# An adaLN block kernel: own PSUM banks in the last product, a one-column 1+ca, a mean shared with ScalarE, and a new order

## Chip, cores and metric

The kernel runs on one core of a Trainium2 chip. The metric is the device time of one launch in microseconds, the median of several runs; lower is better. A core has TensorE (matrix products, PE in the profile), VectorE (DVE), ScalarE (ACT), GpSimd (POOL) and SyncE (SP), which here issues all DMAs from one queue. Each engine works through its own instructions in order and waits at an instruction until what it needs is there. Matrix products write into PSUM, which has eight banks of 512 fp32 columns in each of its 128 partitions.

## What is computed

One transformer block with sequence 2048 and width 512, modulated by a conditioning vector c:

```python
mod = silu(c) @ w_mod                       # six rows: sa, ca, ga, sb, cb, gb
h = layernorm(x) * (1 + ca) + sa
q, k, v = split(h @ wqkv)                   # 32 heads of 16
pq, pk = phi(q), phi(k)                     # phi(t) = where(t > 0, t + 1, exp(t)) + 1e-6
kv, z = einsum(pk, v), sum(pk)              # linear attention: 16 x 16 per head
x = x + ga * ((pq @ kv / (pq @ z)) @ wo)
h = layernorm(x) * (1 + cb) + sb
u = gelu(h @ w_in)                          # 1376 columns: z1 and z2, 688 each
g = w_sp @ layernorm(z2) + b_sp             # mixing along the sequence, 2048 x 2048
x = x + gb * ((z1 * g) @ w_out)
```

## The kernel before

Rows are handled in 16 tiles of 128. Nearly every large operand is split into two halves, a high part rounded to the fast matrix format (fp32r) and a low part, the rest; a product a·b is then three products, high·high, high·low and low·high (mm3, lines 117 to 119). The high part is written by ScalarE, the low part by VectorE or GpSimd. A few small products run in plain fp32, as two instructions each.

The program is a list of short tokens. Two strings, ORDER (first part) and ORDER3 (second part), name some 1,800 steps by two letters and indices; run_all walks through them and emits each step's instructions, DMAs among them, in that order to the engines' queues. Tiles live in numbered slots of pools; the strings in SLOTS say which slot a tile takes at each turn. A step that writes into a slot or a PSUM tile waits until the readers of what was there before are done. A reader and a writer of one PSUM tile wait for each other even where they touch different columns of it.

The steps that matter below, by stage:

- **Start.** load_m (lm), load_wk/load_w (lw), load_xt (ly) and load_x (lx) load the parts of w_mod for sa and ca, the weights, the turned and the plain rows. dummy (du) runs products of ones into a scratch bank. col_mm (cm, line 201) makes 1+ca as a column: 16 fp32 products of 128 x 128 blocks of w_mod with the activated c, spread over 128 columns; col_end (ce) and mean_col (mc, line 333) read it. mean_mm (mr, line 339) makes the mean rows of w_k and w_q over their inputs, four products of 512 columns each, which w_mid (wf, line 343) subtracts from (1+ca)·w. w_hi and w_lo (qh, qd, qg) split the result. k_part (ki, kj, line 424) and k_mm, q_mm (km, qm) are the first products with the split weights; turn_hi and turn_lo (th, tl) split the turned rows. mod_prod and mod_add (yp, ya), then col_part (cr, line 208), make the column of sa, with one-column products.
- **Attention.** gm sums h·pk over all tiles into G. kv_mm and kv_mask (kv, kx) make the masked 16 x 16 blocks. m2_mm (mm0 to mm3, tile pm) multiplies them by wo; two of the four share a PSUM tile, m2_evac (me) takes each out as two halves. a_t and a_te (at, ae) turn and split pq for tiles 0 to 3, wo_mm (wo) is the product po, x1_out (x1) adds it to x.
- **Gated MLP, first product.** h2, then turning by TensorE (ht) or by DMA (hp, hm), splitting (hh, hl), and z_mm (z0, z1, line 661). Tiles 12 to 15 of z1 come late: z_late and z1_late (zw, zg, lines 858 and 864). mod_bcast (mB) makes the last modulation row; mB5 is the last use of the first part's PSUM pools.
- **Mixing along the sequence.** A seven-product scheme over pairs of row blocks: t_diff, t_hi, t_lo and s_sum, s_hi, s_lo (td, th, tl; ss, fh, fl, fg) prepare the operands, prod (pr p,h,k, line 942, tile P) multiplies, c_sum and c_end (cs, cd) combine. u_mul, u_planes, u_x, u_merge, u_sum, u_park (um, up, ux, ug, ua, uq) turn the gated rows and park them in DRAM; u_back, u_hi, u_lo (ur, uh, ul) bring them back and split them.
- **Last product.** Also by seven products for each pair of row blocks p: o_prod (op p,k) and o_rest (or p,n) write four outputs of 256 columns, numbered b,c, by o_mm (line 1127, tile pout); o_add (oa p,n, line 1150) adds them to the rows on VectorE, some of them in the middle of an accumulation (oa p,0 after op p,1; oa p,1 after op p,6; oa p,3 after op p,7; oa p,2 after op p,5), and stores finished rows. The two outputs of one b share a bank; p takes banks 2p+7 and 2p+8, modulo 8. wout_hi and wout_lo (oh, os) split the weights of this product.

The late part's eight banks are given out by bank(k); before, bank k lies at the address of the k-th bank *first used*, zw13's banks 2 and 3 at the first two, where the first part's pool of one-bank tiles "t" lies.

Of the kernel before, what the change touches and what calls it, by code (L numbers as in the profile page):

```python
# [28 lines left out]
def block_kernel(ctx: ExitStack, tc: tile.TileContext, x, x_t, w_qkv, w_o, w_in, w_sp, b_sp, w_out,  # L29
# [166 lines left out]
    def col_mm(m, kc):  # L196
        if m not in CP:
            CP[m] = ps("t", [P, KC, P], f"pcol{m}")
        for i in range(KC):
# [1 line left out]
            mm(CP[m][:, i], RAW["mod", m, kc // 2][:, kc % 2, i * P:(i + 1) * P],
               sil[:, kc:kc + 1].to_broadcast([P, P]), start=n == 1, stop=n == KC * KC, skip_group_check=True)
# [128 lines left out]
    def mean_col():  # L331
        WC["c"] = sb("tb", [P, KC, P], F32, "cbr")
        nc.scalar.activation(WC["c"], CP[1], AF.Copy, scale=1.0 / D, bias=1.0 / D)

    def mean_mm(j, kc):
        if j not in WC:
            WC[j] = ps("t", [P, D], f"wm{j}")
# [1 line left out]
        mm(WC[j], WC["c"][:, kc], w_raw(j, kc), start=n == 1, stop=n == KC)

# [429 lines left out]
    def hx_lo(t):  # L770
# [21 lines left out]
        cr0 qg0,2 ly4 qg0,0 s10 ce0 ly11 kr2 by0 km5 th3 kj1,3 lw2,1 bh0 lx6 s11 bp1 kj0,2 bp3 by1 by2 bp0 qm0
        by3 bp2 ba1 kj0,0 s15 ly6 bx1 lx4 qr0 kr1 tl3 ki0,2 bb1 be1 ka2 ly7 bh1 k15 ba2 kr0 bh2 qm1 ba3 km3
        bx0 lx7 qr1 qm3 ka0 bl0 s13 lw2,0 ka1 lx8 k20 k40 k22 ly8 kr3 kh0 mV2,0 k42 th4 kh2 lx10 bb0 k25 bl2
        lo0 bh3 bh5 ly10 kl0 be0 mV2,1 qm2 ks0 bl1 ly12 tl4 k45 k21 th9 th6 kl2 lx9 ly13 ly14 k41 kh1 ks1 gm0
        bl5 q13 q12 kl1 mS2 bl3 ka3 gm2 th11 tl6 qm4 tl11 kh5 ks2 gm1 lx11 q22 s16 q23 mB2 kl5 tl9 q42 bh6 s14
# [15 lines left out]
        g20 wo5 ht1 hl2 d16 q415 d110 z12 d27 x14 he1 g22 d112 ap7 hm3 z01 lX5 d26 d210 hh3 zl2 g11 am8 ap6
        z02 hl3 h24 d19 g12 z13 ah8 am7 z11 hp4 lX10 am6 ah6 lX8 d212 ah7 g23 g21 al7 x15 zl3 h25 wo7 zl0 z03
        d113 hm4 zn3 lX6 al6 d29 wo6 al8 hh4 ap10 hl4 hp5 d115 zn0 z14 wo8 x17 d213 zh3 x16 ap9 z04 h27 d111
        hm5 zn2 am10 g13 d215 ah10 hh5 ap12 hl5 al10 d211 wo10 hp7 x18 g24 am9 g14 d114 h28 hm7 zl1 z15 x110
# [447 lines left out]
```

## Time and profile before

| | |
|---|---|
| median of 3 runs | 626.55 us (625.43 to 627.54) |
| profiled execution, its own time | 624.86 us |
| its span, first to last instruction | 623.1 us |
| TensorE, busy | 606.1 us (97%) |
| TensorE weight loads, busy | 561.9 us (90%) |
| VectorE / ScalarE / GpSimd, busy | 497.7 / 370.7 / 236.8 us |
| DMA | 109.99 MB, mean 177 GB/s |
| mean granted TensorE clock | 0.993 |

A profile row "PE pm L117 <- DVE m L135: 4.0, 2, 2.5" in the view of waits reads: TensorE's instructions of line 117 that write pm waited for VectorE's instructions of line 135 that write m, 4.0 us in all, 2 times, 2.5 us the longest. In a timeline a row has the start and the duration in us, the engine, line, operation, output and inputs, the shape and the number of instructions; in brackets the idle time before it and what ended it. In the view by groups a row has busy time and mean duration in ns, then the idle time before. In the view by stretches a row has the stretch, its length, then busy time and number of instructions of TensorE, its weight loads, VectorE, ScalarE and GpSimd, and the granted clock, the busy share of the DMA engines and their rate. The chain is what ended last, followed back step by step.

### The profile page before, as it was taken

The numbers are of one execution on the slowest core, as the hardware profiler recorded it, in microseconds if no ns is written. First come the engines' busy times: TensorE is split into PE (matmuls) and PEld (weight loads), VectorE is DVE, ScalarE is ACT, GpSimd is POOL, SyncE is SP. The second block draws the span as 40 slices with busy tenths as digits, with TensorE's granted clock in tenths as the row PEclk, the third lists the DMA queues.
The fourth block names the chain that finished last, engine by engine and source line by source line (L and its number), as shares of the span: only waits on it lengthen the run. The fifth ranks groups of instructions, "written<-read, shape, count | busy, mean of one in ns | idle before, by whom it ended". The sixth has DMA issues, their size and how long they took to land.

```text
span 623.1 us, 9978 instructions
## 1 busy us (share of the span) xinstructions
PE 606.1 (97%) x3542; PEld 561.9 (90%) x3542; DVE 497.7 (80%) x933; ACT 370.7 (59%) x629; POOL 236.8 (38%) x208
## 2 busy tenths in 40 slices
PE   9999999999799999999999999999999999999997
PEld 7688888888589999899999999999999999989997
DVE  2998988896678878898969896866768687998765
ACT  2796594656446564757738455546565667776421
POOL 0842542737865575456422012303121312232320
PEclk9999999999899999999999999999999999999999
DMA  8242520523225546777566926365756848899973
GB/s 324 98 153 85 186 84 23 192 78 125 80 62 147 163 124 193 181 218 240 159 243 234 310 76 188 77 193 143 200 156 174 273 139 231 264 303 259 342 220 120
DMA packets 91027, 109.99 MB, mean 177 GB/s; under 512 B 57088, under 2 KB 57600, under 8 KB 90976
## 3 DMA queue, kind: packets, MB, share of 16 engines
q1 hardware_dynamic: 90976, 109.35, 57.9%
q8 instruction: 28, 0.46, 0.3%
q14 instruction: 23, 0.19, 0.1%
HBM read 68.17 MB, written 28.05 MB: 154 GB/s over the span
## 4 chain that ended last, share of the span: by engine, by line
PE 84%; DMA 5%; DVE 5%; ACT 2%; POOL 2%; issue 1%; SPq 1%; ACTq 0%; POOLq 0%; DVEq 0%
PE P L942 30%; PE z L661 14%; PE pout L1127 9%; PE z L858 2%; PE qp L117 2%; PE qp L118 2%; PE g L119 2%; PE qp L119 2%; PE g L118 2%; PE g L117 2%; PE kp L119 2%; PE kp L117 2%; PE kp L118 2%; PE po L117 2%; PE po L119 2%; PE po L118 2%
## 5 line engine op out<-in xcount | busy, mean ns | idle before, releaser
L942 PE MATMUL P<-z,f 128*128 128x344 f32 x768 | 125.8, 320 | 0.9 <-ACT z L864 0.9
L942 PEld LDWEIGHTS P<-z,f 128*128 128x128 f32 x768 | 121.8, 188 | 1.2 <-ACT z L864 1.1
L929 POOL TENSOR_TENSOR f<-raw_wsp,f 128x512 fp32r<-128x512 f32 x32 | 46.8, 1468 | 170.3 <-ACT f L926 114.6
L661 PE MATMUL z<-win,ht 128*128 128x344 f32 x672 | 107.8, 320 | 0.6 <-DVE ht L305 0.6
L661 PEld LDWEIGHTS z<-win,ht 128*128 128x128 f32 x672 | 106.3, 188 | 1.7 <-DVE ht L305 0.9
L1127 PE MATMUL pout<-wout,ut 128*128 128x256 f32 (+1 forms) x448 | 56.9, 284 | 4.1 <-DVE x L1150 4.0
L1127 PEld LDWEIGHTS pout<-wout,ut 128*128 128x128 f32 (+1 forms) x448 | 54.6, 189 | 5.6 <-DVE x L1150 2.9
L926 ACT ACTIVATE f<-raw_wsp 128x512 fp32r<-128x512 f32 x64 | 39.2, 626 | 29.4 <-PE P L942 20.3
L261 POOL TENSOR_TENSOR mv<-ve,mhalf 128x1 f32<-128x1 f32 x48 | 35.5, 746 | 37.7 <-DVE ve L260 22.0
L926 ACT ACTIVATE f<-sa 128x512 fp32r<-128x512 f32 x48 | 29.8, 628 | 31.1 <-PE P L942 20.5
L929 DVE TENSOR_TENSOR f<-sa,f 128x512 fp32r<-128x512 f32 x48 | 34.2, 719 | 15.2 <-ACT f L926 15.0
L285 ACT COPY uca<-ucb 128x768 uint16<-128x768 uint16 x32 | 32.0, 1069 | 6.6 <-DMA ucb<-uca 6.6
L483 POOL TENSOR_TENSOR pksum<-pksum,tk 128x512 f32<-128x512 f32 x15 | 22.6, 1506 | 34.2 <-DVE tk L455 34.0
L1150 DVE TENSOR_TENSOR x<-x,pout 128x256 f32<-128x256 f32 (+1 forms) x49 | 23.3, 498 | 15.3 <-PE pout L1127 15.1
L1030 ACT ACTIVATE ut<-ur 128x512 fp32r<-128x512 f32 x32 | 18.9, 625 | 22.9 <-DMA ur<-ud 14.9
L590 POOL TENSOR_TENSOR prod<-pq,zrep 128x512 f32<-128x512 f32 x16 | 20.7, 1304 | 22.6 <-DVE den L598 12.0
L929 DVE TENSOR_TENSOR f<-raw_wsp,f 128x512 fp32r<-128x512 f32 x32 | 22.7, 712 | 8.2 <-ACT f L926 8.1
L1039 POOL TENSOR_TENSOR ut<-ur,ut 48x128 fp32r<-48x128 f32 x16 | 11.4, 714 | 43.7 <-ACT ut L1030 43.7
L275 ACT COPY uca<-us 128x768 uint16<-128x768 uint16 x32 | 25.0, 827 | 4.7 <-PE P L942 2.8
L117 PE MATMUL po<-m,pt 128*128 128x512 f32 x64 | 26.1, 408 | 0.0
L119 PE MATMUL po<-m,pt 128*128 128x512 f32 x64 | 25.8, 402 | 0.0
L118 PE MATMUL po<-m,pt 128*128 128x512 f32 x64 | 25.7, 402 | 0.0
(254 smaller groups left out, 1513.6 us busy)
## 6 DMA issues: line engine op xcount, KB each, us to landing
raw_wsp<-in_w_sp SPq DMA_DIRECT2D x32, 512.0 KB, 4.3
ud<-uca SPq DMA_DIRECT2D x16, 512.0 KB, 4.7
ur<-ud SPq DMA_DIRECT2D x16, 512.0 KB, 5.3
z1d<-z SPq DMA_DIRECT2D x16, 344.0 KB, 2.6
zd<-zz SPq DMA_DIRECT2D x16, 344.0 KB, 2.7
z1r<-z1d SPq DMA_DIRECT2D x16, 344.0 KB, 4.1
xt<-in_x_t SPq DMA_DIRECT2D x16, 256.0 KB, 3.8
x<-in_x SPq DMA_DIRECT2D x16, 256.0 KB, 3.3
```

What stands on the lines that cost most here:

```text
L117: mm(o, a_hi, b_hi, start=first, stop=False, **kw)
L118: mm(o, a_hi, b_lo, start=False, stop=False, **kw)
L119: mm(o, a_lo, b_hi, start=False, stop=last, **kw)
L261: nc.gpsimd.tensor_tensor(mv[:, 1:2], ve, mhalf, op=OP.pow)
L275: nc.scalar.copy(pl[:, h], v[:, :, h])
L285: copy(o[:, :, h], plt[:, h * n:(h + 1) * n].rearrange("p a b -> p (a b)"))
L661: mm(p[:, b, :HB], a[:, i, kc], win[h][:, j, kc, b * HB:(b + 1) * HB], start=kc == 0 and k == 0, stop=kc == KC - 1 and k == 2)
L926: nc.scalar.activation(SF[p, h, k][:, 0], s_src(p, h, k), AF.Copy)
L929: eng.tensor_sub(SF[p, h, k][:, 1], s_src(p, h, k), f(SF[p, h, k][:, 0]))
L942: mm(B[p, k][:, :HB], a[:, x_], t[:, y_], start=n == 1, stop=n == 24)
L1127: mm(o_bank(p, b, c), a, w, start=NPO[k] == 1, stop=last, skip_group_check=True)
L1150: nc.vector.tensor_add(o, o, PO[p, b][:, k:k + c1 - c0])
```

## The change

1. 1+ca is made with one column per product instead of 128; mean_col spreads it while reading.
2. The mean row of w_q takes only inputs 0 and 1 (of four blocks) by mean_mm. Blocks 2 and 3 are scaled on ScalarE (ms, mp), added on GpSimd (ma), split (mx) and summed over partitions by two fast products with ones into the same bank (mb).
3. The late part's banks lie in sequence: bank k at address k.
4. Each 256-column output of the last product has a bank of its own: p takes four banks from 4p+7 on, modulo 8. An add of 512 columns becomes two of 256.
5. SLOTS, ORDER and ORDER3 are new. The new steps ms, mp2, mp3, ma2,3, mx2 and mb come in, mr0,2 and mr0,3 go; all other steps are the same, in another order.

```diff
     def col_mm(m, kc):
         if m not in CP:
-            CP[m] = ps("t", [P, KC, P], f"pcol{m}")
+            CP[m] = ps("t", [P, KC], f"pcol{m}")
...
-            mm(CP[m][:, i], RAW["mod", m, kc // 2][:, kc % 2, i * P:(i + 1) * P],
-               sil[:, kc:kc + 1].to_broadcast([P, P]), start=n == 1, stop=n == KC * KC, skip_group_check=True)
+            mm(CP[m][:, i:i + 1], RAW["mod", m, kc // 2][:, kc % 2, i * P:(i + 1) * P],
+               sil[:, kc:kc + 1], start=n == 1, stop=n == KC * KC, skip_group_check=True)
...
-        nc.scalar.activation(WC["c"], CP[1], AF.Copy, scale=1.0 / D, bias=1.0 / D)
+        nc.scalar.activation(WC["c"], CP[1][:, :, None].to_broadcast([P, KC, P]), AF.Copy, scale=1.0 / D, bias=1.0 / D)
...
+    def mean_scale():
+        WC["s"] = const.tile([P, KC], F32, name="cas")
+        nc.scalar.activation(WC["s"], CP[1], AF.Copy, scale=1.0 / D, bias=1.0 / D)
+
+    def mean_prod(kc):
+        WC["p", kc] = sb("tb", [P, D], F32, f"wp{kc}")
+        nc.scalar.activation(WC["p", kc], w_raw(0, kc), AF.Copy, scale=WC["s"][:, kc:kc + 1])
+
+    def mean_add(a, b):
+        nc.gpsimd.tensor_add(WC["p", a], WC["p", a], WC["p", b])
+
+    def mean_split(a):
+        WC["h"] = sb("s4", [P, 2, D], F32R, "wph")
+        hi_lo(WC["h"][:, 0], WC["h"][:, 1], WC["p", a])
+
+    def mean_row():
+        for h in range(2):
+            n = WC["n", 0] = WC["n", 0] + 1
+            mm(WC[0], ones, WC["h"][:, h], start=False, stop=n == KC)
...
     psp = late.enter_context(tc.tile_pool(name="psp", bufs=1, space=PSUM, reuse_waits="tile"))
+    for k in range(8):
+        psp.tile([P, 512], F32, tag=f"bank{k}", name=f"bank_{k}")
...
     def o_bank(p, b, c):
-        if (p, b) not in PO:
-            PO[p, b] = bank((2 * p + 7 + b) % 8, f"pout{p}_{b}")
-        return PO[p, b][:, 256 * c:256 * c + 256]
+        if (p, b, c) not in PO:
+            PO[p, b, c] = bank((4 * p + 7 + 2 * b + c) % 8, f"pout{p}_{b}{c}", (P, 256))
+        return PO[p, b, c]
...
-        nc.vector.tensor_add(o, o, PO[p, b][:, k:k + c1 - c0])
+        for c in range(c0, c1, 256):
+            v = X3[2 * p + t][:, c:c + 256]
+            nc.vector.tensor_add(v, v, PO[p, b, (k + c - c0) // 256])
```

Of the two order strings, the places that the prediction speaks of (old, then new):

```diff
-        lm1,0 lm1,2 lm1,3 du1 du4 si du2 lm1,1 du3 cm1,0 ly1 cm1,2 lw1,0 lw1,1 cm1,3 cm1,1 ce1 ly0 lw0,1 lw0,0
-        du5 lm0,1 mc mr1,1 th1 mr1,0 lm0,0 th0 mr1,3 ly5 ly2 mr1,2 mr0,2 lm0,2 tl1 tl0 mr0,3 wf1,3 wf1,1 wf1,0
-        lm0,3 qh1,3 qh1,1 wf1,2 mr0,0 qg1,3 mr0,1 qh1,0 qd1,0 ki0,1 wf0,1 qg1,1 kj0,3 yp0,1 lx0 ki0,3 wf0,3
+        ly1 lm1,0 lm1,1 du1 du2 du3 si lm1,2 cm1,0 lm1,3 du4 lw1,0 ly5 cm1,1 cm1,2 cm1,3 lw1,1 th1 tl1 du5 ms
+        lw0,1 mc ce1 th5 mp2 lw0,0 mr1,1 ly0 lx0 tl5 mp3 mr1,3 th0 mr1,0 ma2,3 ly2 mr1,2 wf1,3 mr0,0 wf1,2
+        wf1,1 wf1,0 mr0,1 qh1,3 lm0,2 mx2 th2 lx2 tl0 qg1,3 qh1,2 qh1,1 lm0,1 mb qh1,0 qg1,1 lm0,0 s10 yp0,2
...
-        d13 gh0 wh0,3 d22 gh1 d11 gh3 kv0 gh2 d20 d21 kv1 d18 kv3 vb kv2 d23 lX2 at2 wl0,3 wh1,1 kx d28 qm15
-        lX4 q115 d15 at0 qm14 ae0 q114 ae2 mm0 mm2 me0 lW1,2 wh1,0 wl1,0 d14 mm1 at1 me1 me2 mm3 wl1,1 at3 me3
-        wo0 ae3 ae1 d17 d24 wl0,2 ap4 wo3 x10 wh1,2 x13 wo1 wh1,3 w02 wl1,3 h20 ht0 w12 d25 he0 ap5 q215 lX7
+        wh0,2 gh1 gh0 d12 lW1,0 d10 d13 gh3 d22 kv0 gh2 mB4 d20 vb d11 kv3 d23 kv1 lX0 kv2 wh0,3 at2 wh1,1 d18
+        lW1,3 kx qm15 mm2 wl0,3 wl1,1 mm0 at0 ae2 q115 wh1,2 d21 ae0 d14 qm14 d15 wl0,2 me2 me0 at3 mm1 d28
+        q114 mm3 at1 me1 ae1 me3 ae3 wh1,0 wo0 wo3 d24 wh1,3 ap4 wl1,0 x10 x13 wo1 wl1,3 q214 h20 w02 d25 q414
...
-        zp15 tl1,5 zh15 zw12 zp13 tl2,5 ss0,0,4 zt12 zg12 zh12 fh0,1,2 zh13 td0 tl2,6 fh0,0,7 zt14 zg13 zo15
-        th1,6 zh14 fh0,0,3 ss0,1,1 zo13 pr0,0,1 zo12 tl1,6 fh0,1,1 zw14 th1,4 zo14 fl0,0,3 zw15 ts3 fl0,1,1
+        ts0 ss0,0,2 fg0,0,2 th1,5 zn12 fh0,0,6 th1,6 fh0,0,1 zw13 zn13 zl15 td2 fl0,0,6 zp12 th1,4 zw12 zp13
+        zp14 fl0,0,1 ss0,1,3 zh13 zn15 tl1,6 pr0,0,1 ss0,0,4 zw14 zg12 fh0,1,1 zt12 td0 tl1,4 zo13 zt14 zh15
+        zh12 zp15 th2,5 zw15 th0,6 zg13 zh14 zo12 zo15 fh0,0,7 th0,4 fh0,0,5 fl0,1,1 zo14 fh0,0,3 tl0,4
...
-        um14 oh7 ua6,2 up14 ul0 lx2 op0,1 ul1 oa0,0 op0,2 uq13 os5 os8 ua0,4 op0,6 os7 uH0 lz15 ur3 op0,5
-        oa0,1 oa0,2 cd7,4 or0,3 uL0 uh2 or0,0 cs7,0 op0,7 ux14 oa0,3 or0,1 um15 ur4 or0,2 os4 op0,3 ur5 op0,4
+        pr7,1,4 os7 ul0 op0,1 os3 ul1 ur3 oh5 cs7,7 oa0,0 ua0,4 uH0 os5 pr7,0,4 op0,6 ug13 cd7,2 os8 uL0 oa0,1
+        um14 uh3 ua6,3 op0,5 uh2 oa0,2 op0,2 ua6,1 cd7,4 or0,0 or0,3 ur4 uq12 ua6,2 ul3 lz15 cs7,0 ua1,4 op0,7
...
-        op7,6 op7,3 or7,1 oa6,6 oa7,1 op7,7 or7,3 oa7,7 oa7,3 oa7,5 or7,2 op7,4 oa7,4
+        uL7 oa7,2 or7,0 oa7,0 oa6,6 op7,6 or7,1 oa7,1 op7,3 oa7,7 op7,7 or7,3 oa7,3 oa7,5 op7,4 or7,2 oa7,4
```

More of the change, by code (lines that the diff above doesn't have):

```diff
@@ L792, in block_kernel @@
[L792 to L796, printed above, removed]
@@ L812, in block_kernel @@
[L812 to L815, printed above, removed]
-        zp0 ah9 ap11 g25 hh7 al9 lX9 hl7 am12 zn1 zp3 zp2 z05 h26 ah12 al12 d214 wo9 x19 hp6 z07 am11 hp8 zo3
@@ new lines, in block_kernel @@
+        q114 mm3 at1 me1 ae1 me3 ae3 wh1,0 wo0 wo3 d24 wh1,3 ap4 wl1,0 x10 x13 wo1 wl1,3 q214 h20 w02 d25 q414
+        ht0 w12 he0 z00 wl1,2 za0 x12 am4 h22 ap5 ah4 al4 d17 x11 am5 zb0 q215 h23 hp2 g10 ah5 wo4 hm2 al5 d16
+        h21 wo5 hp3 lX10 q415 hh2 lX7 hl2 lX4 d27 g20 ht1 d110 d26 he1 z12 d19 d112 ap7 z01 ap8 hm3 ap6 z02
+        d210 g22 x14 lX6 am7 g11 hh3 ah7 hl3 h24 am8 ah8 z13 al8 z11 am6 d113 d212 g12 al7 d29 ah6 wo7 ap10
+        hp4 g23 x15 zl2 zl3 h25 al6 g21 z03 wo6 x17 am10 hp5 hm4 hh4 d213 ah10 zn2 lX8 hl4 wo8 zl1 x16 h27
@@ L1219, in block_kernel @@
-        or3,0 ur10 or3,1 uh9 oa1,6 ul8 ur11 op4,1 op4,2 ul9 oa2,7 ua4,4 oa3,1 uh10 ur12 op4,5 uH4 oa2,6 op3,7
-        uL3 oa3,3 or3,3 lx10 or4,3 oa4,0 op4,6 op3,4 uh11 oa4,2 oa4,1 uL4 or3,2 ur13 ul10 op3,3 op4,3 op4,7
-        oa3,7 ul11 lx12 or4,1 ua5,4 or4,0 op5,2 uh12 op5,5 oa4,3 uH5 op5,1 uh13 ul12 oa5,0 or5,3 or4,2 uL5
-        op5,6 oa3,6 op6,1 or5,0 ur14 op6,2 oa4,7 oa5,1 uh14 or6,0 lx14 ul13 oa6,0 op4,4 oa4,6 op5,7 op6,6
-        oa5,2 op6,5 ua6,4 oa5,3 op5,3 oa6,1 op5,4 uH6 or5,1 ur15 oa6,2 oa5,7 or5,2 op6,7 lx15 ul14 uL6 or6,3
@@ new lines, in block_kernel @@
+        lx7 up13 os1 oh6 lx0 uh0 lx1 oh3 pr7,0,3 oh8 lx6 pr7,1,3 ux13 os2 pr7,1,2 cs7,5 os6 uh1 cd7,3 ur2 wa4
+        pr7,1,4 os7 ul0 op0,1 os3 ul1 ur3 oh5 cs7,7 oa0,0 ua0,4 uH0 os5 pr7,0,4 op0,6 ug13 cd7,2 os8 uL0 oa0,1
+        um14 uh3 ua6,3 op0,5 uh2 oa0,2 op0,2 ua6,1 cd7,4 or0,0 or0,3 ur4 uq12 ua6,2 ul3 lz15 cs7,0 ua1,4 op0,7
+        uq13 or0,1 op0,3 ur5 ul2 oa0,3 op1,5 or1,3 op1,1 oa1,0 op1,2 oa0,7 uH1 op1,6 or1,0 uL1 oh4 oa1,1 up14
+        or0,2 uh4 os4 oa1,2 op1,7 op0,4 ux14 or1,1 um15 ur7 lx12 oa1,3 ur6 op1,4 or1,2 oa0,6 ur9 uh5 up15 ul4
@@ new lines, in block_kernel @@
+        op2,1 ul5 oa2,0 op2,2 op2,5 op2,6 or2,3 ux15 ua2,4 uH2 op1,3 or2,0 ug14 oa2,1 uh6 oa2,2 or2,1 oa1,7
+        uh7 uL2 ug15 op2,3 ur8 uh8 op2,7 oa1,6 ul6 uh9 op3,1 ul7 oa3,0 ur10 op3,2 oa2,3 lx10 oa2,7 op3,5 op3,6
+        lx13 oa3,1 oa3,2 op2,4 ua7,3 op3,7 ua3,4 or2,2 oa2,6 or3,3 or3,1 ul8 oa3,3 uH3 ul9 or3,0 ua7,1 ua4,4
+        op4,1 uH4 op4,2 op3,4 uL3 or4,0 uq14 oa4,0 op4,5 uh10 ur11 or3,2 op3,3 uL4 ua7,2 oa4,2 op4,3 ul10
+        oa3,7 op4,6 op5,2 ur12 oa4,1 or4,1 or5,0 uh11 uh12 lx15 op5,1 op4,7 oa3,6 ul11 ur13 ua5,4 uq15 op5,5
@@ L1226, in block_kernel @@
+        uH5 oa5,0 oa4,7 oa4,3 op5,6 or4,2 oa5,1 op4,4 or5,3 uL5 oa5,2 ur14 uh13 or4,3 ul12 op5,7 oa4,6 or5,1
+        op5,3 oa5,3 ul13 op6,1 ua6,4 op6,5 or5,2 oa6,0 uH6 uh14 or6,3 oa6,2 ur15 or6,1 op5,4 uL6 oa5,7 oa5,6
+        op6,6 ul14 op6,2 or6,0 op7,1 oa6,1 uh15 op7,2 ul15 op6,7 op6,3 ua7,4 op7,5 oa6,3 uH7 op6,4 or6,2 oa6,7
+        uL7 oa7,2 or7,0 oa7,0 oa6,6 op7,6 or7,1 oa7,1 op7,3 oa7,7 op7,7 or7,3 oa7,3 oa7,5 op7,4 or7,2 oa7,4
     """
```

191 lines of the change are left out of this document (95 added, 96 removed).

## The prediction, made before the change was run

> **What bounds the kernel now.** I read the profile's first part, then what TensorE waited for, then the timelines of the stages where it waited.
>
> ```profile
> span 623.1 us, 9978 instructions
> ...
> PE 606.1 (97%) x3542; PEld 561.9 (90%) x3542; DVE 497.7 (80%) x933; ACT 370.7 (59%) x629; POOL 236.8 (38%) x208
> ```
>
> TensorE (PE) is busy for 606.1 of 623.1 us, so it is the bound nearly everywhere, and all that can be won without dropping products is in its 17.0 idle us and in products that run slowly. The view of TensorE's own waits says who ends them:
>
> ```profile
> PE pm L117 <- DVE m L135: 4.0, 2, 2.5
> PE pout L1127 <- DVE x L1150: 4.0, 6, 1.0
> PE P L942 <- POOL f L929: 1.1, 1, 1.1
> PE warm L179 <- POOL ones L127: 1.0, 1, 1.0
> PE P L942 <- ACT z L864: 0.9, 1, 0.9
> PE z L858 <- ACT mod L247: 0.7, 1, 0.7
> PE kp L119 <- DVE ht L409: 0.7, 1, 0.7
> PE z L661 <- DVE ht L305: 0.6, 1, 0.6
> ```
>
> Two rows carry 4.0 us each: the small products pm (mm0 to mm3) wait for VectorE (DVE) to take an earlier pm out of PSUM, and the last product pout waits for the adds of L1150. Five single waits make 4.0 us more. The rest of the 17.0 is the first microsecond and the tail after the last product. The PE timeline around pm shows that its price is more than the two gaps:
>
> ```profile
> 165.26 0.50 PE L117 MATMUL pm<-wog,kvh 128*128 128x512 f32 x1 [2.47 <-DVE m L135]
> ...
> 168.23 0.79 PE L117 MATMUL pm<-wog,kvh 128*128 128x512 f32 x1 [1.58 <-DVE m L135]
> ...
> 171.39 0.63 PE L119 MATMUL po<-m,pt 128*128 128x512 f32 x1
> 171.81 0.63 PE L117 MATMUL po<-m,pt 128*128 128x512 f32 x1
> ...
> 173.82 0.40 PE L119 MATMUL po<-m,pt 128*128 128x512 f32 x1
> 174.06 0.40 PE L117 MATMUL po<-m,pt 128*128 128x512 f32 x1
> ```
>
> After the second gap products of 512 columns start 0.42 us apart (171.39 to 171.81), after 173.8 they start 0.24 us apart: for 5.59 us, from 168.23 to 173.82, TensorE runs at half rate. At full rate those 11 products and four transposes would take about 11 x 0.24 + 0.3 = 3.0 us. So the place costs 2.47 + 1.58 idle and 2.6 slow, 6.6 us in all.
>
> **The change, part by part.**
>
> *Around pm.* Old list: mm0, mm2, me0, ..., mm1. mm1 writes the other half of the tile that me0 reads, and waits for it; me0's second half stands in DVE's queue behind other work. New list on TensorE: mm2, mm0, at0, qm14, at3, mm1, mm3, at1, wo0. What has to be done under that cover costs, by these two rows (ScalarE's, then VectorE's),
>
> ```profile
> 162.66 0.59 ACT L134 ACTIVATE m<-pm 128x512 fp32r<-128x512 f32 x1
> ```
> ```profile
> 164.52 0.68 DVE L135 TENSOR_TENSOR m<-pm,m 128x512 fp32r<-128x512 f32 x1
> ```
>
> three takings-out (ae0, me2, me0): 0.59 for the first on ScalarE and then 3 x 0.68 on VectorE, 2.6 us, since ae2 can be done earlier. The cover is qm14, 12 x 0.24 = 2.9 us, and at3. So mm1 and mm3 start without a wait, unless DVE has other work in front: q115 and the sum of d21 stand there too and could add 1.3 us, of which 1.0 would show. Late next is me3 for the last quarter of wo0. I leave 1.1 us in place: **-5.5**, ends -6.6 and 0 (the second is a rival, below). The half rate goes with the gaps. The Trainium skill (page "TensorE: Matmul & The Clock Gate", section "Why this matters for your kernels") asks only that gaps above about 3 us be avoided; by it neither gap here would slow the clock, and the change would win about 4.0 and not 6.6 at this place. The rows show the slow steps behind gaps of 2.47 and 1.58, and the measurement decides.
>
> *The last product.* Each pair of row blocks p had two banks, two 256-column outputs in each, and every add of one half held up products into the other half:
>
> ```profile
> 559.14 3.52 PE L1127 MATMUL pout<-wout,ut 128*128 128x256 f32 x26 [1.02 <-DVE x L1150]
> ...
> 586.76 1.46 PE L1127 MATMUL pout<-wout,ut 128*128 128x256 f32 x10 [0.51 <-DVE x L1150]
> 588.73 2.29 PE L1127 MATMUL pout<-wout,ut 128*128 128x256 f32 x17 [0.51 <-DVE x L1150]
> ...
> 618.33 1.58 PE L1127 MATMUL pout<-wout,ut 128*128 128x256 f32 x11 [0.97 <-DVE x L1150]
> ```
>
> Counting instructions along the list from the first op, 586.76 is or3,3 (output 0,1) waiting for oa3,3, which reads output 0,0: a wait that only the shared bank makes. So is 559.14 (or0,3 behind the adds of 0,0), and 588.73 (oa4,0 itself held back by or4,3). 618.33 is op7,4, which truly needs oa7,3, but also waits for oa7,5, a read of the other half. With a bank per output the first three go, and the true ones (op p,6 after oa p,0; op p,7 after oa p,1; op7,4 after oa7,3) have other products between them in the new list: pr7,0,4 before op0,6, or7,3 before op7,4. The price: an add of 512 columns becomes two of 256.
>
> ```profile
> L1150 DVE TENSOR_TENSOR x<-x,pout 128x256 f32<-128x256 f32 x34 | 13.7, 416 | 10.9 <-PE pout L1127 10.7
> ...
> L1150 DVE TENSOR_TENSOR x<-x,pout 128x512 f32<-128x512 f32 x15 | 10.2, 684 | 4.4 <-PE pout L1127 4.4
> ```
>
> 15 x (2 x 416 - 684 ns) = 2.2 us more on DVE, which in this stage idles 15 us waiting for TensorE (10.7 + 4.4), so I cost it at nothing; without that cover it is +2.2. The products themselves keep their size and number. I take **-3.3** of the 4.0, ends -4.0 and -1.8 (4.0 less 2.2). The time after the last product stays: one add, one store.
>
> *The start.* Column products of 1+ca with one column, and w_q's mean with two products on TensorE, two scalings on ScalarE, a sum on GpSimd (POOL), a split, and two products with ones.
>
> ```profile
> 4.56 4.61 PE L201 MATMUL pcol<-sil,raw_mod 128*128 128x128 f32 x32
> ...
> 9.92 7.13 PE L339 MATMUL wm<-raw_qkv,cbr 128*128 128x512 f32 x16 [0.30 <-ACT cbr L333]
> ...
> 25.68 0.95 PE L208 MATMUL pcol<-ones,yp 128*128 128x1 f32 x8
> ```
>
> One-column products exist already: 0.95 us for 8 instructions, so 32 cost at most 3.8 against 4.61, -0.8. A mean product costs 7.13 / 8 = 0.89; two fewer is -1.8, two products of 0.24 come in, -1.3. TensorE sheds 2.1 us. But this stretch waits for loads. The new list puts xt1 before w_ca's columns and xt5 between the halves of w_k, so 2.5 MB stand in SP's queue up to the second half of w_k. In the old list 2.5 MB stood up to xt0, and the chain shows when it landed:
>
> ```profile
> 4.49 6.49 DMA xt<-in_x_t
> ```
>
> At 11.0. So mr1,3 starts at about 11.0 and w_k's mean ends after three products at 13.7, where the old one ended at 9.92 + 4 x 0.89 = 13.5. Behind it, w_q's new row (mb) needs mx2, whose second half stands on DVE behind the four wf's, beside GpSimd work. What that does to such an instruction:
>
> ```profile
> 16.42 1.80 DVE L350 TENSOR_TENSOR wk<-wf,wk 128x512 fp32r<-128x512 f32 x1
> ```
>
> 1.80 us in place of the 0.68 of a like one above. So TensorE, done with mr0,1 at 13.7 + 1.8 = 15.5, waits one to two us for mb and for the first k products: what it sheds it spends waiting. I take **0**, ends -1.0 (cover found) and +1.5 (the stretch falls on tl0 too, which the first k products need).
>
> *Late banks in sequence, and the rest of the order.* Late bank k now lies at address k. zw13 (banks 2 and 3) used to lie on the two early banks of which one held the last modulation product, hence the 0.7 of "z L858 <- ACT mod"; now it lies where the mixer products ended long before. The 0.9 ("P <- ACT z L864") is pr0,0,3 on the bank of zw15; three more products stand before it now. The 1.1 (f) and 0.6 (ht) hang on order alone. That is 3.3 (the fifth, 0.7 of kp, belongs to the start). Against it, some 1,800 positions have moved, and a new list has its own waits: zw14, for one, now stands in front of zg12, which empties its banks. I take **-0.5**, ends -3.3 and +1.5.
>
> Sum: -5.5 - 3.3 + 0 - 0.5 = -9.3. The profiled execution took 624.86 us (623.1 of span and 1.8 around it), 1.7 below the median of 626.55; it would take 615.6, and the median **617.3**. All the good ends together make -6.6 - 4.0 - 1.0 - 3.3 = -14.9, or 611.7.
>
> **Rivals.**
> 1. *VectorE holds the gain back.* Between the two stages lies one in which DVE is nearly full:
>
> ```profile
> 250.00:280.00 30.00, 29.39 (x164) 26.96 (x163) 27.64 (x64) 19.78 (x34) 15.67 (x16) 1.00 0.79 202
> ```
>
> 27.64 of 30 us. If DVE can't deliver the turned rows earlier, TensorE runs into it and gives back the 5.5: 622.8. Against it: most of what DVE does there is released by TensorE's own products, which come earlier too.
>
> 2. *The half rate had another cause than the gaps* and stays at this place: 2.6 less, 619.9. The rule of the Trainium skill quoted above ("TensorE: Matmul & The Clock Gate") would lead here.
>
> 3. *The banks change nothing* because the waits were for the adds in any case: 3.3 less, 620.6. Against it: at 586.76 the next product doesn't touch what the add reads.
>
> 4. *Slower: the ring of banks is too short.* Two p now fill all eight banks, where four p did. op2,1 needs the bank that oa0,6 reads; between op0,4 and op2,1 stand 16 instructions, at 3.52 / 26 = 0.135 us 2.2 us of cover. It decides as soon as DVE trails TensorE by more. With a lag of 3.7 us each p from 2 to 7 waits 1.5, 9 us; the last product then wins nothing, the rest 6.0: 629.6. For it: DVE got the first adds done 1.0 us late at 559.14. Against it: its 15 idle us in this stage.
>
> 5. *No change*: 1 and 3 together, and new waits in the moved order eat the rest: 626.
>
> **How the numbers follow.** Forecast 0.55, rival 1 0.15, rival 2 0.05, rival 3 0.07, rival 4 0.10, rival 5 0.08. A measurement of this kernel tells 0.3%, 1.9 us, from no change. Faster: the forecast, 2, 3 and most of 1 (0.13), 0.80; same: 5 and the rest of 1, 0.10; slower: 4, 0.10. The range begins at 611.7, where every good end is reached, and ends at 624.0, past rivals 1 to 3; 4, 5 and the worst of 1 stay outside, under 2 in 10.
>
> **What would show it.** Right: no wait of pm for DVE m, products 0.24 us apart from pm on, no wait of pout above 0.5 us, mixer products of the first row blocks some 6 us earlier against the start of the k products, busy TensorE time down by 4 to 5 us (2.1 of the start, 2.6 of slow steps). Wrong: a wait of z for DVE ht or xph between 180 and 300 of several us (rival 1), pout waiting for DVE x at op p,1 (rival 4), a wait of the first kp above 2 us (the start), or steps of 0.42 us at another place.

## The result, and the profile after

The kernel after takes **617.65 us** (median of six, 614.57 to 620.24), the kernel before 626.88 (625.43 to 629.98): a ratio of **0.985**, 95% interval 0.981 to 0.989. A second set of six gave 619.13 against 627.07 for the kernel before, ratio 0.989 (0.986 to 0.992). The forecast was 617.3, range 611.7 to 624.0. The profiled execution is the fastest of the first six, 614.57, with a span of 612.8.

First the head of the page of after:

```profile
span 612.8 us, 9999 instructions
...
PE 604.7 (99%) x3540; PEld 560.7 (92%) x3540; DVE 508.4 (83%) x949; ACT 374.6 (61%) x633; POOL 246.5 (40%) x209
```

The span is 10.3 us shorter, but TensorE (PE) is busy for only 1.4 us less; the prediction expected 4 to 5. So the gain is almost all idle time, and somewhere TensorE must be working more slowly than before. The view of TensorE's waits in after is short (us in total, times, longest):

```profile
PE P L964 <- DVE f L951: 1.1, 1, 1.1
PE pcol L201 <- DMA raw_mod<-in_w_ca: 1.1, 1, 1.1
PE warm L179 <- POOL tiny L131: 1.0, 1, 1.0
PE wm L358 <- DVE wph L135: 0.9, 1, 0.9
PE z L880 <- ACT z L886: 0.4, 1, 0.4
PE wm L358 <- ACT wph L134: 0.3, 1, 0.3
```

Neither pm nor pout is in it: the two rows of 4.0 us are gone. Three of the six are new and belong to the start. The PE timeline around pm in after:

```profile
164.58 0.60 PE L311 MATMUL tpp<-ident,pq 128*128 128x128 f32 x4
164.94 0.49 PE L117 MATMUL pm<-wog,kvh 128*128 128x512 f32 x1
...
166.79 0.48 PE L117 MATMUL po<-m,pt 128*128 128x512 f32 x1
167.10 0.39 PE L118 MATMUL po<-m,pt 128*128 128x512 f32 x1
167.33 0.40 PE L119 MATMUL po<-m,pt 128*128 128x512 f32 x1
```

There is no gap, and the steps are 0.23 us (167.10 to 167.33): the half rate went with the gaps. The groups of the last product, first the products in before, then products and adds in after:

```profile
L1127 PE MATMUL pout<-wout,ut 128*128 128x256 f32 x384 | 53.6, 284 | 4.1 <-DVE x L1150 4.0
```
```profile
L1149 PE MATMUL pout<-wout,ut 128*128 128x256 f32 x384 | 52.0, 283 | 0.1
...
L1174 DVE TENSOR_TENSOR x<-x,pout 128x256 f32<-128x256 f32 x64 | 24.3, 413 | 7.9 <-PE pout L1149 7.6
```

The idle time ahead of the products fell from 4.1 to 0.1 us; the adds, now all of 256 columns, still wait 7.6 us for TensorE, so their extra work on VectorE (DVE) is covered. It is also less than the 2.2 us that the prediction took: 24.3 us busy in place of 13.7 + 10.2 = 23.9.

The start is what went wrong. The PE timeline of after, from the first column product:

```profile
4.97 1.02 PE L201 MATMUL pcol<-sil,raw_mod 128*128 128x1 f32 x8 [1.06 <-DMA raw_mod<-in_w_ca]
...
6.38 4.17 PE L201 MATMUL pcol<-sil,raw_mod 128*128 128x1 f32 x24
...
11.41 6.79 PE L338 MATMUL wm<-raw_qkv,cbr 128*128 128x512 f32 x12
...
20.23 1.94 PE L443 MATMUL kp<-wk,ht 128*128 128x512 f32 x7
```

A product of this kind is two instructions, and the counts behind the x are of instructions. The first eight of them take 0.13 us each, the other 24 take 0.17 in the mean. The view of windows says why (the granted clock is the third column from the right):

```profile
6.00:7.00 1.00, 1.00 (x11) 1.00 (x11) 0.00 (x0) 0.00 (x0) 0.00 (x0) 1.00 1.10 350
7.00:8.00 1.00, 1.00 (x8) 1.00 (x8) 0.00 (x0) 0.00 (x0) 0.00 (x0) 0.71 0.97 367
8.00:9.00 1.00, 1.00 (x6) 1.00 (x6) 0.00 (x0) 0.00 (x0) 0.00 (x0) 0.50 1.06 418
...
14.00:15.00 1.00, 1.00 (x3) 0.46 (x2) 0.00 (x0) 0.63 (x1) 0.78 (x1) 0.88 1.05 391
```

From 7.4 to 14.2 us the clock is at half speed although TensorE is never idle there (1.00 busy in each window).

With five instructions that stand in both timelines as border posts, the two spans part as follows (us; cr0 is the product of eight one-column instructions at L208, behind the same products in both lists):

| stretch | before | after | difference |
|---|---|---|---|
| to cr0 | 25.68 | 27.61 | +1.93 |
| cr0 to the first pkv | 125.51 | 125.01 | -0.50 |
| first pkv to the first tph | 30.52 | 23.94 | -6.58 |
| first tph to the last pmod | 142.22 | 141.58 | -0.64 |
| last pmod to the first pout | 230.54 | 229.11 | -1.43 |
| first pout to the end of the last | 65.44 | 62.40 | -3.04 |
| from there to the span's end | 3.19 | 3.15 | -0.04 |

Two groups of products crossed a post: mB4's two (0.47 us) went behind the first pkv, and the twelve of pr7,0,4 (1.9 us) behind the first pout. Allowing for them, the stretches are worth about 0, -7.0, -0.6, +0.5 and -4.9.

### The profile page after: what moved, and what is told of

It reads as the page before. It is cut to its first block, busy times and chain, and to the rows that moved or that the text cites. A ratio compares the mean times of both kernels' runs of the same rounds, so it can differ in the third digit from the quotient of the medians.

```text
span 612.8 us, 9999 instructions
## 1 busy us (share of the span) xinstructions
PE 604.7 (99%) x3540; PEld 560.7 (92%) x3540; DVE 508.4 (83%) x949; ACT 374.6 (61%) x633; POOL 246.5 (40%) x209
## 4 chain that ended last, share of the span: by engine, by line
PE 89%; DVE 5%; DMA 2%; ACT 2%; issue 1%; SPq 0%; DVEq 0%; ACTq 0%
PE P L964 31%; PE z L681 17%; PE pout L1149 9%; PE po L119 2%; PE po L117 2%; PE po L118 2%; PE qp L117 2%; PE qp L119 2%; PE qp L118 2%; PE g L119 2%; PE g L118 2%; PE g L117 2%; PE kp L118 2%; PE kp L119 2%; PE kp L117 2%; PE z L880 1%
## 5 line engine op out<-in xcount | busy, mean ns | idle before, releaser
L260 POOL TENSOR_TENSOR mv<-ve,mhalf 128x1 f32<-128x1 f32 x48 | 39.1, 822 | 54.4 <-DVE ve L259 34.9
L1174 DVE TENSOR_TENSOR x<-x,pout 128x256 f32<-128x256 f32 x64 | 24.3, 413 | 7.9 <-PE pout L1149 7.6
L951 DVE TENSOR_TENSOR f<-raw_wsp,f 128x512 fp32r<-128x512 f32 x32 | 24.3, 762 | 4.0 <-ACT f L948 4.0
L117 PE MATMUL qp<-wq,ht 128*128 128x512 f32 x64 | 25.5, 398 | 0.1
L117 PE MATMUL po<-m,pt 128*128 128x512 f32 x64 | 25.4, 396 | 0.0
L119 PE MATMUL po<-m,pt 128*128 128x512 f32 x64 | 25.2, 394 | 0.0
L118 PE MATMUL g<-pkhl,hhl 128*128 128x512 f32 x64 | 25.2, 393 | 0.0
```

Source lines behind the costliest of these rows:

```text
L117: mm(o, a_hi, b_hi, start=first, stop=False, **kw)
L118: mm(o, a_hi, b_lo, start=False, stop=False, **kw)
L119: mm(o, a_lo, b_hi, start=False, stop=last, **kw)
L260: nc.gpsimd.tensor_tensor(mv[:, 1:2], ve, mhalf, op=OP.pow)
L951: eng.tensor_sub(SF[p, h, k][:, 1], s_src(p, h, k), f(SF[p, h, k][:, 0]))
L1174: nc.vector.tensor_add(v, v, PO[p, b, (k + c - c0) // 256])
```

## The experiments

Theory: the gains at pm and in the last product are the removed waits, and the start loses because one-column products keep TensorE's clock down. Rivals: the new order as such made the gains; the start loses by its loads or by its one gap. "The first" and "the second kernel" below mean before and after.

**Columns of 128 in the second kernel (s_col128).**

```diff
-            mm(CP[m][:, i:i + 1], RAW["mod", m, kc // 2][:, kc % 2, i * P:(i + 1) * P],
-               sil[:, kc:kc + 1], start=...
+            mm(CP[m][:, i], RAW["mod", m, kc // 2][:, kc % 2, i * P:(i + 1) * P],
+               sil[:, kc:kc + 1].to_broadcast([P, P]), start=...
```

> The kernel after, with the 32 column products of 1+ca 128 columns wide again, as in the kernel before; the order stays. Theory A: it is the one-column products that let the granted clock fall to 0.50 from 7.4 to 14.3 us. Then the clock stays at 1.00, the twelve mean products of L338 take about 5.4 us in place of 6.79, and the first one-column product of the bias (cr0) starts up to 2 us earlier than 27.61, at 25.6 to 26.6; the whole is 1 to 2 us shorter. Theory B: it is the idle 1.06 us at 3.9, where the first column product waits for raw_mod behind xt1. Then the clock falls as before, and cr0 stays at 27.6. Theory C: the loads of w_k and w_q set the start whatever the clock. Then the clock stays at 1.00 and cr0 stays within 0.5 us of 27.6.

Measured: 614.23 us (612.51 to 614.77), ratio to before 0.979 (0.976 to 0.982); cr0 at 25.33. Its PE timeline:

```profile
5.00 1.13 PE L201 MATMUL pcol<-sil,raw_mod 128*128 128x128 f32 x8 [1.09 <-DMA raw_mod<-in_w_ca]
...
6.42 2.84 PE L201 MATMUL pcol<-sil,raw_mod 128*128 128x128 f32 x24
9.10 0.61 PE L179 MATMUL warm<-ones 128*128 128x128 f32 x4
10.08 5.81 PE L338 MATMUL wm<-raw_qkv,cbr 128*128 128x512 f32 x12 [0.37 <-ACT col L213]
```

The gap of 1.09 is still there and the loads are the same; the 24 instructions, 128 times as wide, take 2.84 us in place of 4.17, and the mean 5.81 in place of 6.79. Theory A holds; B (the gap) and C (the loads) fall. cr0 came 0.3 us earlier than A's range, and the median is 3.4 below that of after, where 1 to 2 were expected. At 0.118 us each the wide instructions cost as much as one-column ones at full clock (0.95 / 8 = 0.119 at cr0): the narrow form saves nothing even then.

**One column in the first kernel (b_onecol).** The same edit the other way round, alone.

> The kernel before, with only the column products of 1+ca made one column wide; its order, its loads and its mean of four products stay. Theory A: the granted clock falls to 0.50 between 7 and 9 us, the mean products that come next run at half rate for some microseconds, cr0 starts 0.7 to 2 us later than the 25.68 of the kernel before. Theory B: no gap, so the clock stays at 1.00, the columns take 3.8 us or less in place of 4.61, and cr0 starts at 25.0 to 25.7. The whole moves by no more than 2 us either way.

Measured: 628.98 us (626.29 to 633.3), ratio 1.004 (1.002 to 1.007), so slower, by 3.1 us in the medians, where no more than 2 was expected; cr0 at 29.84, 4.2 us later, where 0.7 to 2 was expected. Its PE timeline:

```profile
4.56 6.83 PE L201 MATMUL pcol<-sil,raw_mod 128*128 128x1 f32 x32
11.24 1.20 PE L179 MATMUL warm<-ones 128*128 128x128 f32 x4
12.24 8.97 PE L338 MATMUL wm<-raw_qkv,cbr 128*128 128x512 f32 x16
```

The four dummy instructions of L179 are the reader's gauge: 1.20 us here, 0.61 in the rows of the experiment above, for the same instructions. TensorE has been busy without a pause since 0.98 us, and the clock is still down at 12 us. The windows show 1.00 as granted clock for this whole stretch: they know of no change before the first one that was recorded (full clock from 16.1 us on), so at a start the clock is read from the steps.

The gauge gives the same answer in every profile of this document: right behind the columns the four dummies take 1.20 us in all five with one-column products and 0.61 in all nine with wide ones. The traces' records of the clock agree: full clock begins at 4.5 to 10.4 us with wide columns, at 15.3 to 18.4 with one column, and in after, where it came up at 4.0 and fell at 7.4, for good at 14.2.

**The other order of loads (s_loads).**

```diff
-        ly1 lm1,0 lm1,1 du1 du2 du3 si lm1,2 cm1,0 lm1,3 du4
+        lm1,0 lm1,1 du1 du2 du3 si lm1,2 cm1,0 lm1,3 ly1 du4
```

> The kernel after, with the load of xt1 behind the four loads of w_ca for 1+ca in place of ahead of them; one-column products stay. Theory A (one-column products lower the clock): the gap of 1.06 us goes, the clock still falls to 0.50, cr0 starts at 26.5 to 27.2 in place of 27.61. Theory B (the gap lowers the clock): the clock stays at 1.00, cr0 at 25.6 to 26.2. Theory C (loads set the start): cr0 at 27.6 or later, since w_k comes later by nothing and xt1 by 2 us.

Measured: 618.04 us (616.53 to 619.57); cr0 at 29.01. The gap fell to 0.55 us, and the columns took 1.83 and 5.12 us, at half rate from the first. A's number and B's were not met, A's because a clock that stayed down from the first column on was not thought of. C's (27.6 or later) was, but its reason was not: the time is in columns at half rate and not in longer waits for loads. B falls: without most of the gap the clock is worse.

**The second kernel once more (after_again), and with wide columns beside it (c_best).**

> The kernel after once more, unchanged, to see which of its times is the usual one. Theory A (its one-column products leave the clock down for most of the start; the profiled 614.57 was the lucky one of six): the median lies at 617 to 619; in the profile the columns of L201 take some 7 us in all, as in the kernel with the other order of loads (1.83 and 5.12), and cr0 starts at 29 to 30.5, not at 27.61. Rival (the start of the profiled run is the usual one, and the spread of the times comes from elsewhere): cr0 at 27 to 28 again.

> The kernel after with 128-column products of 1+ca, in the same rounds as the kernel after. Theory A: 3 to 4.5 us faster than it, 613.5 to 615, with a narrower spread. Rival (half of the gain seen before was luck of the runs): 1 to 2 us faster.

Measured: 619.13 us (616.2 to 621.31) and 615.99 (612.42 to 618.19); the mean differs by 2.9 us, just under theory A's 3 to 4.5, and 615.99 lies above its 613.5 to 615. Over both sets of each kernel (12 and 10 runs) it differs by 3.2, with an interval of about 1.4 to 5.0. The PE timeline of after_again:

```profile
5.10 1.84 PE L201 MATMUL pcol<-sil,raw_mod 128*128 128x1 f32 x8 [1.19 <-DMA raw_mod<-in_w_ca]
...
7.80 5.12 PE L201 MATMUL pcol<-sil,raw_mod 128*128 128x1 f32 x24
...
13.77 7.69 PE L338 MATMUL wm<-raw_qkv,cbr 128*128 128x512 f32 x12
```

cr0 at 30.86: theory A of after_again holds, a little past the ends of its ranges (619, 30.5), and 614.57 was the lucky one. But the start costs the end less than it costs cr0: 3.25 us later there than in the profiled run of after, 1.57 later at the first pout (548.82 against 547.25). From the last pmod to the first pout it takes 227.95 us, in after 229.11, in s_col128 230.51, while its waits of P for VectorE's f are 0, 1.1 and 2.7: whoever comes early waits there. That fits these three; a_pmback below comes latest of all and still waits 1.4, so it isn't the whole rule. For the same reason c_best won less than the 3.4 between s_col128 and after, and its own columns started cold too:

```profile
5.12 2.05 PE L201 MATMUL pcol<-sil,raw_mod 128*128 128x128 f32 x8 [1.21 <-DMA raw_mod<-in_w_ca]
...
7.81 3.81 PE L201 MATMUL pcol<-sil,raw_mod 128*128 128x128 f32 x24
...
12.44 5.42 PE L338 MATMUL wm<-raw_qkv,cbr 128*128 128x512 f32 x12 [0.37 <-ACT col L213]
```

The expected narrower spread didn't come. But the clock is up by the mean (5.42), where after_again's is not (7.69).

**Wide columns and the other order of loads (s_both).** Both edits above.

> The kernel after with 128-column products of 1+ca (614.23 us), and the load of xt1 behind the four loads of w_ca for 1+ca. Theory A (with a clock that is up, the columns bound the start): they start 0.5 us earlier, cr0 starts 0.3 to 0.6 us earlier than 25.33. Theory C (the loads of w_k and w_q bound it): the total of bytes ahead of w_k is the same, so cr0 stays within 0.3 us. Against both: the clock comes up later, as the columns start before TensorE has been busy long enough, and cr0 is 1 us later or more.

Measured: 614.37 us (613.75 to 615.0), ratio 0.981 (0.979 to 0.983); cr0 at 25.42. The columns start at 3.93, 1.07 us earlier than in s_col128, and cr0 doesn't move: the mean now waits 0.52 us for w_k's load. C holds here: with the clock up, the loads set the start.

**w_q's mean on TensorE again (c_mean4).** With wide columns; products mr0,2 and mr0,3 come back, and the scalings, sum, split and row of ones go:

```diff
-        ... du5 ms lw0,1 mc ce1 th5 mp2 lw0,0 mr1,1 ly0 lx0 tl5 mp3 mr1,3 th0 mr1,0 ma2,3 ly2 ...
-        wf1,1 wf1,0 mr0,1 qh1,3 lm0,2 mx2 th2 lx2 tl0 ... lm0,1 mb qh1,0
+        ... du5 lw0,1 mc ce1 th5 lw0,0 mr1,1 ly0 lx0 tl5 mr1,3 th0 mr1,0 ly2 ...
+        wf1,1 wf1,0 mr0,1 mr0,2 mr0,3 qh1,3 lm0,2 th2 lx2 tl0 ... lm0,1 qh1,0
```

> The kernel after with 128-column products of 1+ca (614.23 us), and w_q's mean by four products on TensorE again; the two scalings, the sum, the split and the two products with ones are gone. Theory A of the prediction (what TensorE sheds it spends waiting): TensorE does 1.3 us more and waits 1.3 us less (0.37 and 0.89 at L358), so that the first one-column product of the bias (cr0) starts within 0.5 us of 25.33, the whole within 1 us. Rival (the shift to ScalarE wins as meant): cr0 starts 1 to 1.5 us later. Other rival (the shift costs, since VectorE and GpSimd are what the first k products wait for): cr0 starts 0.7 us earlier or more.

Measured: ten times in two groups, four from 612.33 to 614.67 and six from 620.0 to 622.94. The lower group (median 613.4) lies where s_col128 lies (614.2), so the shift is worth nothing to the whole. In its profile, one of the upper group, cr0 (27.16) can't be compared, as raw_mod landed 0.7 us later and the columns ran cold. From the first mean product to the first k product it takes 12.94 to 19.71, 6.77 us, against 7.46 in c_best (7.90 in s_col128, whose mean products themselves took 0.4 longer, 5.81 against 5.42): the shift to ScalarE costs 0.7 us there, and the last rival is nearest.

The upper group is a matter of its own. DVE's timeline in that profile, then GpSimd's (POOL):

```profile
158.63 6.24 DVE L758 TENSOR_TENSOR kvm<-kvm,mask 128x512 f32<-128x512 f32 x1
```
```profile
157.56 1.33 POOL L610 TENSOR_TENSOR prod<-pq,zrep 128x512 f32<-128x512 f32 x1
158.83 1.07 POOL L622 TENSOR_TENSOR pq<-pq,den 128x512 f32<-128x512 f32 x1
159.85 1.29 POOL L610 TENSOR_TENSOR prod<-pq,zrep 128x512 f32<-128x512 f32 x1
161.09 3.24 POOL L560 TENSOR_TENSOR win<-raw_win,win 128x688 fp32r<-128x688 f32 x2
169.06 1.06 POOL L622 TENSOR_TENSOR pq<-pq,den 128x512 f32<-128x512 f32 x1 [4.73 <-DVE den L620]
```

One VectorE instruction of 0.78 us took 6.24, and ended 0.54 us after GpSimd's chain (161.09 + 3.24 = 164.33; 158.63 + 6.24 = 164.87). pm waited 5.0 us for ScalarE's split of its result, and half rate followed.

**The same with a shorter chain on GpSimd (m4_wl).**

```diff
-        kx qm15 mm2 wl0,3 wl1,1 mm0 ... at3 mm1 d28
+        kx qm15 mm2 mm0 ... at3 mm1 wl0,3 wl1,1 d28
```

> The kernel with 128-column products of 1+ca and w_q's mean by four products, whose ten times fell in two groups (612.3 to 614.7 and 620.0 to 622.9), with two sums of w_in on GpSimd moved some places later, behind mm1. In the profile of the slow group the product of kvm with the mask on VectorE took 6.24 us in place of 0.78 and ended 0.5 us after a chain of eight GpSimd instructions without a pause between them. Theory A (VectorE's instruction gets no access while GpSimd's instructions follow each other): the chain is shorter by 3.2 us, so the instruction takes 3 us at most, and no time lies above 619. Rival (chance, or the loads): the two groups stay as they are.

Measured: 622.62 us (619.64 to 623.97). DVE's and GpSimd's timelines:

```profile
157.18 3.05 DVE L758 TENSOR_TENSOR kvm<-kvm,mask 128x512 f32<-128x512 f32 x1
```
```profile
158.40 1.29 POOL L610 TENSOR_TENSOR prod<-pq,zrep 128x512 f32<-128x512 f32 x1
```

The instruction is 3.2 us shorter, as the chain is, and again ends 0.54 us after it (159.69 and 160.23): the hold-up lasts as long as the chain. The claim on the times failed: no run was below 619, since pm still waits 1.8 us, with half clock behind it, and po now waits 2.2 for VectorE's xr.

The chain alone doesn't make the hold-up, though. In after GpSimd is busy without a pause as well (14.00 us of the 14 from 155 to 169), and the same instruction goes through (VectorE's row, then GpSimd's):

```profile
158.02 0.79 DVE L758 TENSOR_TENSOR kvm<-kvm,mask 128x512 f32<-128x512 f32 x1
```
```profile
156.96 1.30 POOL L610 TENSOR_TENSOR prod<-pq,zrep 128x512 f32<-128x512 f32 x1
158.21 1.52 POOL L622 TENSOR_TENSOR pq<-pq,den 128x512 f32<-128x512 f32 x1
```

It starts 1.06 us behind the start of GpSimd's prod; in c_mean4 that is 1.07 us and in m4_wl 1.08. Here GpSimd's next instruction pays, with 1.52 us in place of 1.07; there VectorE's pays, with the rest of the chain. So it is two outcomes of nearly the same meeting. What decides between them is open, and so is whether they make the two groups of c_mean4, whose lower group left no profile.

**qm14 back ahead of mm2 (a_pmback).**

```diff
-        kx qm15 mm2 ... mm0 at0 ae2 q115 wh1,2 d21 ae0 d14 qm14 d15
+        kx qm15 qm14 mm2 ... mm0 at0 ae2 q115 wh1,2 d21 ae0 d14 d15
```

> The kernel after, with the twelve products of qm14 put back ahead of mm2, as in the old list; nothing else moves. Theory A (the cover of qm14 is what freed pm): TensorE waits for VectorE's m again, 3 to 4 us in one or two gaps, the granted clock falls to 0.50 behind them, and the stretch from the first pkv product to the first transpose tph grows from 23.94 by 5.5 to 6.6 us; the whole is 5 to 7 us longer, about 623. Rival (it was the new order on VectorE, me2 ahead of me0, and the rest of the list): the gaps come to under 1 us and the stretch grows by less than 1.5 us. Between them: the gaps come back and the clock stays at 1.00, then 3 to 4 us.

Measured: 623.36 us (621.12 to 625.87). Its PE timeline:

```profile
164.20 0.50 PE L117 MATMUL qp<-wq,ht 128*128 128x512 f32 x1 [1.54 <-DVE tq L453]
...
171.66 0.50 PE L117 MATMUL pm<-wog,kvh 128*128 128x512 f32 x1 [2.17 <-DVE m L135]
172.00 0.39 PE L118 MATMUL pm<-wog,kvh 128*128 128x512 f32 x1
172.23 0.40 PE L119 MATMUL pm<-wog,kvh 128*128 128x512 f32 x1
```

Gaps of 1.54 and 2.17 us, steps of 0.23 behind them, and pkv to tph 28.06 us (155.22 to 183.28), 4.1 more than in after: the case between the two theories. Only the gap of 2.17 is pm's; the other is qm14's own, which at its earlier place waits for VectorE to read an earlier qp. pm's gap, over the 1 us that the rival allows, says that the cover of qm14 is what freed pm.

**The order around pm alone, in the first kernel (b_pmcover).**

```diff
-        at0 qm14 ae0 q114 ae2 mm0 mm2 me0 lW1,2 ... mm1 at1 me1 me2 mm3
+        at0 ae0 ae2 mm0 mm2 qm14 me0 me2 q114 lW1,2 ... mm1 at1 me1 mm3
```

> The kernel before, with only the order around pm changed as the kernel after has it: mm0, mm2, then the twelve products of qm14, me0 and me2 next in VectorE's list ahead of q114, then mm1 and mm3. Theory A (qm14 under the taking-out frees 2.47 and 1.58 us and the half rate behind them): the stretch from the first pkv product to the first transpose tph shrinks from 30.52 to 24 or 25.5 us, steps stay at 0.23 to 0.24 us throughout, and the whole is 5 to 6.6 us shorter, 619.3 to 621. Rival 1 of the prediction (VectorE holds the gain back later): the stretch shrinks as much, but the whole by less than 2 us. Rival 2 (the half rate has a cause of its own): steps of 0.42 us stay, the stretch shrinks by about 4.

Measured: 621.63 us against 625.65, ratio 0.993 (0.990 to 0.995); pkv to tph 25.53 (152.79 to 178.32), 5.0 less. Steps stay at 0.23. The gain stays to the end (4.0 of 5.0), against rival 1. What is late next is new:

```profile
161.74 0.50 PE L117 MATMUL pm<-wog,kvh 128*128 128x512 f32 x1 [1.54 <-ACT kvh L134]
```

With qm14 gone from ahead of mm0, mm0 comes too early for the split of kvm. In after that product on VectorE (L758; L738 in this kernel) starts at 158.02, not at 159.93, and nothing waits.

**Two banks for each p in the new list (c_oldbanks).** With wide columns; o_bank and o_add as in the first kernel.

> The kernel after with 128-column products of 1+ca (614.23 us), and the last product in two banks for each p again, two outputs in each, adds of 512 columns whole; the order stays the new one. Theory A (the shared bank makes the waits): TensorE waits for VectorE at pout again, 3 to 5 us in some six gaps; from the first pout to the last product it takes 62.5 to 64.5 us in place of 59.4, and the whole is 617 to 619.5. Rival (the new order alone does it, the banks change nothing, rival 3 of the prediction): under 1 us of waits, the whole within 1 us of 614.2.

Measured: 621.19 us (618.8 to 622.33). From the first pout to the end of the last it takes 549.62 to 615.57, 65.95 us, against 62.36 in s_col128: 3.6 more. Its waits:

```profile
PE pout L1149 <- DVE x L1172: 3.5, 3, 2.0
```

A holds at this place, with 3.5 us in three gaps, not six. One of the three, 0.97 us, is op7,4's at 614.00; in after, with the same order, it is gone. (The 59.4 of the expectation runs to the start of the last row of s_col128's timeline, at 606.07.) The whole is above A's 617 to 619.5. Its span is 6.5 above that of s_col128: besides these 3.6 its cr0 came 1.4 later, qp waited 0.9, and from the last pmod to the first pout it took 0.7 more (231.25 against 230.51), which isn't the banks. The own banks under the old list weren't tried: there a product of p + 2 (op6,1) stands ahead of one that the last add on its bank needs (op4,4).

**Late banks not in sequence (c_noseq).** With wide columns, without the loop over bank_0 to bank_7.

> The kernel after with 128-column products of 1+ca, and without the loop that puts the eight late banks at addresses in sequence. Theory A (the prediction's: the 0.7 us wait of z for ScalarE's mod came from a late bank on the bank of the last modulation product): in this look z waits 0.5 to 1 us for ScalarE's mod again, right behind the last modulation product. Rival (the new order alone took it away): no such wait. The time is one look, and says nothing below 2 us.

Measured, in a single run: 614.87 us. Its PE timeline right behind the last modulation product:

```profile
319.84 5.46 PE L878 MATMUL z<-win,ht 128*128 128x344 f32 x33 [0.75 <-ACT mod L246]
```

The wait of 0.7 is back where it was in before, and no other profile with the new list has it, so the addresses took it away.

## Why the prediction was right, point by point

**pm, -5.5 taken, -6.6 to -7.0 measured.** Right in mechanism, near its good end. Nothing of the 1.1 us left in place stayed. a_pmback and b_pmcover give 4.1 (1.5 of it another wait) and 5.0 us for this place by itself.

**The half rate.** Rival 2 is out: in after it went with the gaps. But neither a gap nor its length makes it. In before, gaps of 2.47 and 1.58 us lie 1.4 us of work apart, and the clock falls; in a_pmback gaps of 1.54 and 2.17 lie 5.3 us of work apart, and it stays; in m4_wl a lone gap of 1.76 brings half clock and a lone one of 2.21 doesn't. The traces' records of the clock show the pattern: within a run its changes lie 3.41 us or whole multiples of that apart (in before it is down from 166.81 to 173.64, 6.83 us). Two stretches of m4_wl and one of before on that grid:

```profile
158.88:162.30 3.42, 1.66 (x6) 0.78 (x5) 2.67 (x4) 1.78 (x3) 0.81 (x1) 1.00 0.00 0
...
175.95:179.37 3.42, 1.63 (x7) 1.36 (x8) 2.48 (x6) 2.58 (x5) 2.08 (x2) 1.00 0.24 93
```
```profile
163.40:166.81 3.41, 1.40 (x7) 0.98 (x7) 1.80 (x3) 1.07 (x3) 3.41 (x3) 1.00 0.78 258
```

The clock fell at the end of the first and the third and stayed behind the second. Over all fourteen profiles, from cr0 to the last product, full clock ended behind five such stretches, with TensorE busy for 0.09 to 1.66 us, and went on behind all others, with 1.63 us or more: the border is near half of the stretch. So the busy share of a stretch fits them all, and it matters how the gaps fall on the grid. One-column products seem hardly to count as busy: in after the clock fell behind 4.00 to 7.41, with 2.44 us busy, and stayed down through 7.41 to 10.83, with all of it busy. The Trainium skill's warning ("TensorE: Matmul & The Clock Gate", section "Why this matters for your kernels") names idle gaps above about 3 us; the rows of before show half rate with none that long.

**The last product, -3.3 taken, -4.9 measured.** 3.6 of it are the banks (c_oldbanks); the other 1.3 came with the rest of the new list and weren't isolated. Rival 3 fell, and so did rival 4: in after no product of p + 2 waits for an add. One reading of the prediction was off by a place: by the count of instructions 618.33 is or7,2, which writes the same output as op7,4; and or7,3 stands ahead of the two in the old list as well, so that the new order adds no cover there.

**The start, 0 taken (-1.0 to +1.5), +1.9 in the profiled run and +5.2 in after_again.** This is the step that failed. "32 cost at most 3.8 against 4.61, -0.8" set a one-column price from a place at full clock against a 128-column price from a place where the clock was still coming up, and took the clock as given. From start to start an instruction takes, in both widths, 0.112 us at full clock (s_col128's columns, and cr0's) and 0.213 at half (c_best's first columns, and b_onecol's); the narrow ones cost more in the end because the clock doesn't come up during them. The mean's "what it sheds it spends waiting" was right, with 0.7 us more spent than shed.

**Late banks and the rest of the order, -0.5 taken.** 0.7 by the addresses alone (c_noseq). Of the five single waits one remains (P for f, 1.1, now VectorE's f), and a new one of 0.4 came (z for ScalarE's z). The stretch up to the first pout is 0.5 slower for reasons not found.

**Rivals 1 and 5.** No change (5) is outside the interval of the ratio. Rival 1 is small here: in b_pmcover 4.6 of the 5.0 us are still there from cr0 to the last pmod (293.67 us against 298.25), but an early start is partly given back in the P stage.

**The sum.** -9.3 was forecast; the medians differ by 9.2, in the second set by 7.9. That it is so close is luck: two terms better than taken and one worse came out even, and the start alone moved cr0 by 1.9 in one profile and by 5.2 in the other. PE's busy time is the sign that told: -1.4 in place of -4 to -5, and -3.9 in s_col128 (602.2), where the clock is up early.

## What to carry to other kernels

Price an operation at the clock at which it will run: products that get narrower at the start can hold the clock down for those behind them, and the time of a fixed dummy instruction shows it where the clock column doesn't. Where a small product waits for its tile to be emptied, put independent products of the length of that emptying between them; that was worth more here than all else. Give outputs that are read at different times their own banks, and move the list along with them.
